# GpSimd's low halves of q and k, subtracted in three pieces of 192 columns

## The chip, the core and the metric

The kernel runs on one core of a Trainium2 chip. The core has a matrix engine (TensorE; PE in the profile, and PEld for its weight loads), three engines for elementwise work (VectorE or DVE, ScalarE or ACT, GpSimd or POOL) and SyncE (SP), which issues most of the transfers. Each runs its own instructions in program order and waits on semaphores for the others. The metric is the device time of one execution in microseconds; less is better.

## What is computed

Three layers follow each other; the change lies in the first, an attention with a decay of 4 x 8 heads, 576 positions and 64 columns a head:

```
scores = scale * np.matmul(q, k.transpose(0, 1, 3, 2))
log_f = np.log(np.clip(f, 0.0001, 1.0))
cum = np.cumsum(log_f, axis=-1)
decay = cum[:, :, :, None] - cum[:, :, None, :]
causal = np.triu(np.ones((S, S), dtype=bool), k=1)
scores = np.where(causal, -1000000000.0, scores + decay)
scores = scores - np.max(scores, axis=-1, keepdims=True)
attn = np.exp(scores)
attn = attn / (np.sum(attn, axis=-1, keepdims=True) + 1e-09)
return np.matmul(attn, v).astype(np.float32)
```

Its output goes through a mix over positions and a feed-forward layer (512 to 2048 to 512), and through a second attention of four experts of which each position uses two.

## The kernel before

The 32 heads of the first attention are done in 16 pairs, one head to a slot. Products on TensorE take operands in two parts, a high one and what it leaves out (the low one), and add three products. ScalarE rounds q and k of a head to the high part (L895 to L899); GpSimd subtracts it from the value (L950 in `split_low`: `qb` for q, then `kb` for k, each 64 partitions by 576 columns), and SyncE's queue copies parts to the other partitions. The values lie in one of two places, `aside` (even pairs) and `room` (odd pairs), that are loaded again (L877) once the subtractions have read them. The parts are made a pair ahead of their use.

In a head's slot TensorE computes scores (`sc`, L297), in a first part and a second one of three column groups; ScalarE takes exponentials (L317, into `pf` or a part of `aside`) and rounds them to the high part `ph` (L322), VectorE subtracts for the low one (L325). From the eleventh head on GpSimd sets the exponentials above the diagonal to zero in between (the selections, L1076), five a head; in the heads before, a product adds a mask. For the head after next TensorE computes products `ua` and `ub` (L201, L219), whose row maxima VectorE finds (L206, L227: once on `ua`, four times on `ub`); TensorE turns them (`mt`, L233), ScalarE shifts them (`mr`, L239) and the queue writes them as a row of the operand (L243). `ub` uses the PSUM buffers of `sc`, so it waits until the exponentials have been read from them. Products of the feed-forward layer (`hps`, `cps`) fill TensorE's time between.

The order on every engine is written out by a table of times: each step is put at a time of a slot of 8.4 units, the steps are sorted, and each engine's instructions are issued in that order, GpSimd's too. The times only set the order; on the chip an instruction starts when its engine has got to it and its semaphores allow. The steps of a pair's parts:

```
us = 4.9 if h else SLOT + 2.8
put(h, us, split_high, p, j)
put(h, us + 1.2, split_moves, p, j)
put(h, us + 1.2, split_low, p, j)
```

and those of a head's exponentials (time of the exponential, of the high part, of the low part):

```
for n, (te, th, tl) in enumerate(((0.75, 2.3 if select else 1.35, 2.7),
                                  (2.2, 3.35, SLOT + 0.4), (2.75, 4.3, SLOT + 1.15))):
```

So the low parts of the second and third group come in the next slot, behind its row maxima.

Of the kernel before, what the change touches and what calls it, by code (L numbers as in the profile page):

```python
# [15 lines left out]
OP = mybir.AluOpType  # L16
# [3 lines left out]
B, H, S, D = 4, 8, 576, 64  # L20
# [58 lines left out]
def f32(ap):  # L79
    return ap.bitcast(F32)  # L80
# [3 lines left out]
def kernel(  # L84
# [13 lines left out]
    nc = tc.nc  # L98
# [773 lines left out]
    def pair_heads(p):  # L872
        return heads[2 * (p % 2)], heads[2 * (p % 2) + 1]
# [64 lines left out]
    def split_low(p, j, which=(0, 1)):  # L938

        if p >= NPAIR:  # L940
            return
        qa, qb, ka, kb = pair_heads(p)[j]
        tq, tk = places[p % 2][0][:, 0, :], places[p % 2][0][:, 1, :]
        if j == 0:
            todo = ((qb[hi_, :], tq[lo_], qa[lo_, :]), (kb[lo_, :S], tk[lo_], ka[lo_, :S]))
        else:
            todo = ((qb[lo_, :], tq[hi_], qb[hi_, :]), (kb[hi_, :S], tk[hi_], khigh[hi_, :]))
        for n in which:
            dst, src, high = todo[n]
            nc.gpsimd.tensor_tensor(dst, src, f32(high), OP.subtract)  # L950

    def one(gen):

# [229 lines left out]
    def split_events(p):  # L1183

        for j in range(2):
            if p < 2:
                for us, do in zip(FIRST_SPLITS[2 * p + j], (split_high, split_moves, split_low)):
                    early(us, do, p, j)
                continue
            h = 2 * (p - 2) + j  # L1190
# [4 lines that stand above are left out]
        if p < 2:  # L1195
            early((1.2, 5.0)[p], load_qk, p)
            early((1.7, 8.6)[p], load_v, p)
            put(0, (0.9, 6.5)[p], load_second, p)
            for j in range(2) if p else ():
                early((10.65, 14.3)[j], put_sums, p, j)  # L1200
            return
        put(*((2 * (p - 2) - 1, 0.1) if p > 2 else (0, -0.05)), load_qk, p)
        put(2 * (p - 2), 2.0 if p > 2 else 8.1, load_v, p)
        if p < NPLAIN:
            put(2 * p - 1, 4.6, load_second, p)
# [964 lines left out]
```

## Time and profile before

| what | value |
|---|---|
| median of 3 runs | 785.31 us (784.35 to 785.93) |
| the profiled execution, its own time | 784.53 us |
| its span (first to last instruction) | 782.8 us |
| around the span | 1.73 us |
| TensorE busy | 757.9 us, 97% of the span |
| GpSimd busy | 202.9 us, 26% of the span |
| first attention | about 10 to 250 us of the span |
| subtractions of L950 | 64, of which 60 from the second pair on |

The profile is of one execution. Busy time is the time in which an engine had an instruction under way, matmuls overlap each other, and their ends are modelled.

### The profile page before, as it was taken

The numbers are of one execution on the slowest core, as the hardware profiler recorded it, in microseconds if no ns is written. First come the engines' busy times: TensorE is split into PE (matmuls) and PEld (weight loads), VectorE is DVE, ScalarE is ACT, GpSimd is POOL, SyncE is SP. The second block draws the span as 40 slices with busy tenths as digits, with TensorE's granted clock in tenths as the row PEclk, the third lists the DMA queues.
The fourth block names the chain that finished last, engine by engine and source line by source line (L and its number), as shares of the span: only waits on it lengthen the run. The fifth ranks groups of instructions, "written<-read, shape, count | busy, mean of one in ns | idle before, by whom it ended". The sixth has DMA issues, their size and how long they took to land.

```text
span 782.8 us, 19114 instructions
## 1 busy us (share of the span) xinstructions
PE 757.9 (97%) x7312; PEld 645.3 (82%) x7312; DVE 601.8 (77%) x1662; ACT 436.4 (56%) x892; POOL 202.9 (26%) x357
## 2 busy tenths in 40 slices
PE   8898989999999999999999999999999999999997
PEld 4798989989999999877777777777778888878874
DVE  8989999999999859988773685466644688787763
ACT  7689888878787635644331242113312466786663
POOL 9842566666564200000020000000000611111110
PEclk9999999999999999999999999999999999999999
DMA  6667765665663166835223124200103475343322
GB/s 191 185 192 202 219 176 167 184 175 169 178 191 97 64 202 205 260 126 168 67 86 129 54 89 157 107 1 2 62 31 77 120 185 139 77 118 97 92 76 95
DMA packets 65688, 101.97 MB, mean 130 GB/s; under 512 B 8854, under 2 KB 43644, under 8 KB 65596
## 3 DMA queue, kind: packets, MB, share of 16 engines
q1 hardware_dynamic: 65084, 99.49, 43.3%
q8 instruction: 58, 0.95, 0.5%
q10 hardware_dynamic: 512, 1.25, 0.5%
q14 instruction: 34, 0.28, 0.1%
HBM read 53.25 MB, written 23.74 MB: 98 GB/s over the span
## 4 chain that ended last, share of the span: by engine, by line
PE 51%; DVE 3%; ACT 1%; DMA 1%; issue 0%; SPq 0%; ACTq 0%
PE cps L732 17%; PE hps L716 16%; PE pq L1668 6%; PE pv L1712 3%; PE sc L297 3%; PE po L1764 2%; PE ub L219 1%; PE av L353 1%; PE av L357 1%; PE av L355 1%; DMA ust<-udram 1%; PE pos L1764 1%; PE ua L201 0%; DVE ph L325 0%; DVE uam L588 0%
## 5 line engine op out<-in xcount | busy, mean ns | idle before, releaser
L721 ACT ACTIVATE hh<-hps 128x288 f16<-128x288 f32 (+1 forms) x128 | 52.4, 410 | 210.7 <-PE hps L716 185.7
L722 DVE SCALAR_TENSOR_TENSOR hl<-hps,hh 128x288 f16<-128x288 f32 (+1 forms) x128 | 58.2, 454 | 79.5 <-ACT hh L721 79.2
L227 DVE CUSTOM_DVE_ANT_0 ub<-ub,maskm 128x448 f32<-128x448 f32 x192 | 82.3, 429 | 1.8 <-PE ub L219 0.3
L297 PE MATMUL sc<-qa,ka 128*128 128x288 f32 (+4 forms) x288 | 72.0, 310 | 0.0
L738 DVE SCALAR_TENSOR_TENSOR yc<-cps,back,yc 128x288 f32<-128x288 f32 x96 | 49.3, 514 | 24.6 <-PE cps L732 23.0
L297 PE MATMUL sc<-qb,kb 128*128 128x288 f32 (+4 forms) x288 | 63.5, 302 | 0.0
L353 PEld LDWEIGHTS <-ph 128*128 128x128 f16 x645 | 58.9, 97 | 1.2 <-DVE o L434 0.6
L355 PEld LDWEIGHTS <-ph 128*128 128x128 f16 x645 | 59.3, 98 | 0.2
L357 PEld LDWEIGHTS <-ph 128*128 128x128 f16 x645 | 59.3, 97 | 0.0
L1896 POOL TENSOR_SCALAR_AFFINE_SELECT pf<-pf 128x128 f32<-128x128 f32 (+1 forms) x80 | 23.8, 318 | 116.4 <-ACT pf L317 115.8
L297 PEld LDWEIGHTS sc<-qb,kb 128*128 128x128 f32 x288 | 52.3, 188 | 1.5
L325 DVE TENSOR_TENSOR ph<-pf,ph 128x512 f16<-128x512 f32 (+1 forms) x66 | 47.5, 732 | 6.4 <-ACT ph L322 6.4
L206 DVE CUSTOM_DVE_ANT_0 ua<-ua,maskm 128x576 f32<-128x576 f32 x48 | 36.5, 761 | 18.8 <-PE ua L201 12.1
L325 DVE TENSOR_TENSOR ph<-aside,ph 128x512 f16<-128x512 f32 (+1 forms) x63 | 50.7, 817 | 0.1
L297 PEld LDWEIGHTS sc<-qa,ka 128*128 128x128 f32 x288 | 48.8, 190 | 2.0 <-issue 0.4
L317 ACT ACTIVATE aside<-sc 128x512 f32<-128x512 f32 (+1 forms) x63 | 38.7, 618 | 20.4 <-PE sc L297 16.9
L1076 POOL TENSOR_SCALAR_AFFINE_SELECT aside<-aside 128x128 f32<-128x128 f32 (+1 forms) x80 | 39.9, 518 | 38.3 <-ACT aside L317 28.8
L732 PE MATMUL cps<-hh,w16b 128*128 128x288 f16 x256 | 48.3, 286 | 0.3 <-DVE hl L722 0.3
L732 PE MATMUL cps<-hh,w1lf 128*128 128x288 f16 x256 | 48.4, 286 | 0.0
L732 PE MATMUL cps<-hh,w16a 128*128 128x288 f16 x256 | 48.4, 286 | 0.0
L317 ACT ACTIVATE pf<-sc 128x512 f32<-128x512 f32 (+1 forms) x66 | 39.8, 610 | 13.0 <-PE sc L297 9.4
L732 PEld LDWEIGHTS <-w16b 128*128 128x128 f16 x384 | 37.4, 98 | 10.2 <-issue 0.8
(289 smaller groups left out, 2469.5 us busy)
## 6 DMA issues: line engine op xcount, KB each, us to landing
raw<-in_w_dram SPq DMA_DIRECT2D x32, 512.0 KB
ust<-udram SPq DMA_DIRECT2D x13, 576.0 KB
ydram<-yc SPq DMA_DIRECT2D x10, 576.0 KB
aside<-in_qk_dram SPq DMA_DIRECT2D x8, 576.0 KB
udram<-ustage SPq DMA_DIRECT2D x16, 288.0 KB
ydram<-ust SPq DMA_DIRECT2D x8, 576.0 KB
yc<-ydram SPq DMA_DIRECT2D x8, 576.0 KB
room<-in_qk_dram SPq DMA_DIRECT2D x7, 576.0 KB
```

The costliest lines, as they stand in the source:

```text
L227: nc.vector.tensor_tensor_reduce(ub[:, bk, off:off + w], ub[:, bk, off:off + w], maskm[:, S - w:S], 1.0, NEG, OP.add, OP.max, mx[:, t:t + 1])
L297: nc.tensor.matmul(ps[:, bk, off:off + w], wa, xa, start=bk not in banks[:n], stop=bk not in banks[n + 1:])
L317: nc.scalar.activation(pf[:, 0:S].rearrange("p (c n) -> p c n", c=2) if whole else pf[:, 0:n], view, AF.Exp, scale=ISC)
L325: nc.vector.tensor_tensor(pl[:, o0:o0 + n], pf[:, 0:n], ph[:, o0:o0 + n], OP.subtract)
L353: nc.tensor.matmul(av[:, it, :], ph[:, c:c + P], vh[:, jt, :], start=first, stop=False)
L355: nc.tensor.matmul(av[:, it, 0:64], ph[:, c:c + P], vl[:, jt, :], start=False, stop=False)
L357: nc.tensor.matmul(av[:, it, :], pl[:, c:c + P], vh[:, jt, :], start=False, stop=last)
L716: nc.tensor.matmul(ph[:], wa[:, k, fs], xa[:, k], start=n == 0, stop=n == 3 * KT - 1)
L721: after(lambda: nc.scalar.activation(hh[:], ph[:], AF.Relu), lambda: nc.vector.scalar_tensor_tensor(hl[:], ph[:], 0.0, high, OP.max, OP.su ...
L722: lambda: nc.vector.scalar_tensor_tensor(hl[:], ph[:], 0.0, high, OP.max, OP.subtract))
L732: nc.tensor.matmul(pc[:], wa[:, t, dsl], xa[:], start=n == 0, stop=n == 3 * FT - 1)
L738: nc.vector.scalar_tensor_tensor(yc[:, d, :], pc[:], back, yc[:, d, :], OP.mult, OP.add)
```

## The change

From the second pair on (`p` not 0) each subtraction of 576 columns is issued as three of 192, one behind the other, over the same rows. The first pair keeps its four whole ones. So 60 instructions become 180.

```
+        w = S // 3 if p else S
         for n in which:
             dst, src, high = todo[n]
-            nc.gpsimd.tensor_tensor(dst, src, f32(high), OP.subtract)
+            for c in range(0, S, w):
+                nc.gpsimd.tensor_tensor(dst[:, c:c + w], src[:, c:c + w], f32(high[:, c:c + w]),
+                                        OP.subtract)
```

On GpSimd, in the slots of the heads with selections, there stood before (names of buffers, then partitions and columns):

```order
L950 TENSOR_TENSOR qb_135<-room,qa_134 64x576
L950 TENSOR_TENSOR kb_137<-room,ka_136 64x576
L1076 AFFINE_SELECT aside<-aside 128x128 x3
L1076 AFFINE_SELECT pf<-pf 128x128
L1076 AFFINE_SELECT pf<-pf 128x64
L950 TENSOR_TENSOR qb_139<-room,qb_139 64x576
L950 TENSOR_TENSOR kb_141<-room,khigh 64x576
```

and now, at the same place, with every line number behind the change three higher:

```order
L952 TENSOR_TENSOR qb_135<-room,qa_134 64x192 x3
L952 TENSOR_TENSOR kb_137<-room,ka_136 64x192 x3
L1079 AFFINE_SELECT aside<-aside 128x128 x3
L1079 AFFINE_SELECT pf<-pf 128x128
L1079 AFFINE_SELECT pf<-pf 128x64
L952 TENSOR_TENSOR qb_139<-room,qb_139 64x192 x3
L952 TENSOR_TENSOR kb_141<-room,khigh 64x192 x3
```

Nothing moved past anything else: the six pieces stand where the two subtractions stood, ahead of the same selections.

On TensorE, in the second part of a head's scores, the order is the same and two products have got a wait of their own, since they read columns of later pieces than the first part did:

```order
L297 MATMUL sc<-qa_138,ka_140 128x448
L297 MATMUL sc<-qb_139,kb_141 128x320 [waits Pool_49]
L297 MATMUL sc<-qb_139,kb_141 128x192 [waits Pool_49]
L297 MATMUL sc<-qb_139,kb_141 128x448
L297 MATMUL sc<-qa_138,ka_140 128x64
```

Before, these rows stood without a wait, since the first part had waited for the whole tile.

## Rows read from the trace of the kernel before

**Rows 1.** Stretches: us, busy of PE, PEld, DVE, ACT, POOL, clock, DMA.

```profile
18.00:120.00 102.00, 94.14 (x970) 85.57 (x968) 95.49 (x282) 84.68 (x172) 56.62 (x57) 1.00 0.69 197
120.00:240.00 120.00, 116.06 (x1353) 110.66 (x1352) 114.78 (x323) 96.08 (x190) 75.76 (x99) 1.00 0.60 174
```

**Rows 2.** Waits of weight loads, 18 to 280 us: total, times, longest.

```profile
PEld mt L233 <- DVE mx L227: 11.6, 20, 1.6
...
PEld ub L219 <- ACT aside L317: 3.3, 4, 1.3
```

**Rows 3.** VectorE's waits, 0 to 250 us: total, times, longest.

```profile
DVE ua L206 <- PE ua L201: 6.8, 12, 1.0
```

**Rows 4.** VectorE in order of time: start us, us.

```profile
29.63 0.39 DVE L461 SCALAR_TENSOR_TENSOR u<-ur,u 128x160 int32<-128x160 int32 x1
30.05 1.46 DVE L462 SCALAR_TENSOR_TENSOR u<-ur,u 128x160 int32<-128x160 int32 x1
31.43 1.72 DVE L407 SCALAR_TENSOR_TENSOR vw<-room,rs,vw 128x320 f16<-128x320 f32 x1
...
34.33 0.74 DVE L325 TENSOR_TENSOR ph<-aside,ph 128x576 f16<-128x576 f32 x1
```

**Rows 5.** GpSimd in order of time, the same stretch.

```profile
29.91 1.41 POOL L950 TENSOR_TENSOR qb<-aside,qb 64x576 fp32r<-64x576 f32 x1
31.40 1.41 POOL L950 TENSOR_TENSOR kb<-aside,khigh 64x576 fp32r<-64x576 f32 x1
...
34.18 2.17 POOL L950 TENSOR_TENSOR qb<-room,qa 64x576 fp32r<-64x576 f32 x1
```

**Rows 6.** VectorE elsewhere, with no subtraction on GpSimd beside it.

```profile
74.74 0.55 DVE L407 SCALAR_TENSOR_TENSOR vw<-aside,rs,vw 128x320 f16<-128x320 f32 x1
...
201.06 0.68 DVE L325 TENSOR_TENSOR ph<-aside,ph 128x512 f16<-128x512 f32 x1
```

**Rows 7.** GpSimd, one slot with selections.

```profile
137.91 1.40 POOL L950 TENSOR_TENSOR qb<-room,qb 64x576 fp32r<-64x576 f32 x1 [1.50 <-issue]
139.39 1.42 POOL L950 TENSOR_TENSOR kb<-room,khigh 64x576 fp32r<-64x576 f32 x1
140.89 0.63 POOL L1076 TENSOR_SCALAR_AFFINE_SELECT aside<-aside 128x128 f32<-128x128 f32 x1
...
143.21 0.48 POOL L1076 TENSOR_SCALAR_AFFINE_SELECT aside<-aside 128x128 f32<-128x128 f32 x2
```

**Rows 8.** VectorE: low parts behind `kb`, in that slot and two others.

```profile
51.91 1.08 DVE L325 TENSOR_TENSOR ph<-pf,ph 128x512 f16<-128x512 f32 x1
...
140.28 1.08 DVE L325 TENSOR_TENSOR ph<-aside,ph 128x512 f16<-128x512 f32 x1
...
141.28 0.77 DVE L325 TENSOR_TENSOR ph<-aside,ph 128x512 f16<-128x512 f32 x1
...
243.09 1.06 DVE L325 TENSOR_TENSOR ph<-aside,ph 128x512 f16<-128x512 f32 x1
```

**Rows 9.** Groups of GpSimd's instructions by shape: count, busy us, mean ns.

```profile
L950 POOL TENSOR_TENSOR kb<-aside,ka 64x576 fp32r<-64x576 f32 x8 | 11.3, 1412 | 0.6
...
L1076 POOL TENSOR_SCALAR_AFFINE_SELECT aside<-aside 128x64 f32<-128x64 f32 x15 | 4.0, 264 | 0.0
...
L1300 POOL TENSOR_TENSOR vs<-vst,vs 32x288 fp32r<-32x288 f32 x2 | 1.6, 794 | 2.8 <-ACT vs L1296 2.7
```

**Rows 10.** GpSimd, first selections of two other slots.

```profile
116.52 0.28 POOL L1076 TENSOR_SCALAR_AFFINE_SELECT aside<-aside 128x128 f32<-128x128 f32 x1
...
243.67 0.63 POOL L1076 TENSOR_SCALAR_AFFINE_SELECT aside<-aside 128x128 f32<-128x128 f32 x1
```

**Rows 11.** ScalarE and TensorE in the slot of the 140.28 low part.

```profile
141.96 0.66 ACT L322 CAST ph<-aside 128x576 f16<-128x576 f32 x1
142.52 0.60 ACT L317 ACTIVATE aside<-sc 128x512 f32<-128x512 f32 x1
...
143.19 0.74 PE L219 MATMUL ub<-ka,qa 127*128 127x448 f32 x4
```

## Prediction

> **What bounds the kernel now.** The page's busy shares are averages over stages, so I read the stage of the change by itself, in the busy times by stretch. In the first attention VectorE is as full as TensorE: 95.49 of 102 us and 114.78 of 120 us, where TensorE has 94.14 and 116.06; GpSimd has 56.62 and 75.76 [rows 1]. What the change is worth is made there and then passed on, since none of its 60 subtractions stands behind 245 us and the engines' order behind them is the same.
>
> Then the waits. TensorE waits chiefly for VectorE: 20 times and 11.6 us for the last row maximum; four times and 3.3 us it waits for ScalarE's exponentials to free the buffer of `ub` [rows 2]. VectorE in turn waits 12 times, 6.8 us in all, for the products of `ua` [rows 3], one product group to each of 32 heads. The two run in step. GpSimd is not full, but what it does holds the others in two ways, which the next parts show from the rows in order of time.
>
> **What a subtraction does to VectorE.** At 29.63 an integer operation L461 takes 0.39 us; L462, of the same shape, starts at 30.05 and takes 1.46 [rows 4]. GpSimd's `qb` runs from 29.91 to 31.32 [rows 5], and L462 ends at 31.51, 0.19 us behind it. The next one, L407, takes 0.55 us in a free place [rows 6] and 1.72 here: GpSimd's `kb` came in at 31.40, and L407 ends 0.34 us behind its end at 32.81. At 140.28 a low part L325 takes 1.08 us instead of 0.68 and ends at 141.36, 0.55 us behind `kb` [rows 6, 7, 8]. The reading: a VectorE operation with two inputs in SBUF does its last part, about 0.2 to 0.55 us by its length, only when GpSimd's subtraction is over; and when GpSimd has another ready, the two take turns, one instruction each. [...]
>
> **The price of a piece.** No L950 of 192 columns is in the trace. Two shapes of the same operation are: 576 columns take 1412 ns, 288 take 794 [rows 9]. That is 618/288 = 2.15 ns a column and 176 ns for each instruction, so 192 columns take 588 ns. Two selections that follow each other, of 128 and of 64 columns, take 0.48 us together [rows 7], where one of each apart takes 0.28 [rows 10] and 0.26 [rows 9]; so I let a next piece start 0.05 early: 0.588 + 2 x 0.54 = 1.67 us for three, 0.26 more than one whole, 0.52 for `qb` and `kb`. Bounds: no price at all for an instruction (0.47 a piece, nothing added), and the 0.07 us that lie between `qb` and `kb` [rows 5] ahead of each piece (0.66 a piece, 0.5 added for each three). I take the middle one, since the 288 columns are the nearest row.
>
> **Early slots, where something is gained.** I work through the turns from 29.91. The first piece ends at 30.50, so L462 ends 0.19 behind it, at 30.69 instead of 31.51. The second piece takes its turn, of which VectorE sees some 0.45 us, and L407 ends 0.34 behind it, at 31.48 instead of 33.15: 1.67 us gained. But four pieces are left, and two of the next operations of VectorE have two inputs in SBUF again, another L462 and the low part of 34.33 [rows 4]; before, they ran with no subtraction beside them. Each waits for a piece, 2 x 0.45, and 0.77 us are left. What TensorE waits for most are maxima that stand behind such operations on VectorE [rows 2], so I let TensorE gain all of it: **-0.8** (bounds: nothing, and -1.67).
>
> **Low parts that come behind `kb`.** From 51.9 to 243.1 us there are 14 places where a low part of the second group, or the low part of the feed-forward input, is held behind `kb`; the first, the last and the one at 140.28 are shown [rows 8], and in all 14 the held operation starts within 1 us of `kb`'s start, as there by 0.89 [rows 7]. I work through the one of `qb` at 137.91 [rows 7]. `qb` in pieces ends at 139.58, `kb` begins at 139.65, its second piece runs to 140.78. The low part ends 0.55 behind that, at 141.33, where it ended at 141.36: nothing is gained, since the pieces have pushed `kb` back. The third piece takes its turn from 141.33 to 141.78, and now the second low part, which took 0.77 right behind the first [rows 8], has to wait: it ends 0.55 behind the piece, at 142.33 instead of 142.05. VectorE is 0.28 us later, where it should be earlier. VectorE's own idle time swallows it in 12 of 32 heads [rows 3]; in 9 of the 14 places (five belong to the next part) I count 9 x 0.28 x 20/32 = **+1.6** (bounds: 0, and 9 x 0.45 = 4).
>
> **Selections that come right behind `kb`.** The first selection at 140.89 stands right behind `kb` and ended at 141.52 [rows 7]. In pieces, and behind the second low part, it ends at about 142.48, 0.96 later. ScalarE's rounding of that group began at 141.96 [rows 11], so 0.44 is covered and ScalarE is 0.52 late; queued behind it is the exponential of 142.52, and when that ended at 143.12 TensorE's `ub` could start at 143.19. There is no slack in that chain: `ub` goes to about 143.7. Of the 18 slots with both subtractions and selections, 7 have no gap between `kb` and the selection, the first at 116.52 and the last at 243.67 [rows 10]; the others have gaps that hide some or all of it. TensorE would have waited for the next maximum in most heads anyway [rows 2], and that maximum is itself only 0.28 late; so each of the 7 costs between 0.28 and 0.52, and I take 0.35: **+2.45** (bounds: 0, and 7 x 0.96 = 6.7).
>
> **What costs nothing.** TensorE's new waits are for pieces made a head or more before. The queue's load of `room` or `aside` waits for the same subtractions and comes up to 1 us later, with the row of the maxima behind it on the same queue; that row waits longer for ScalarE in the slots I looked at. If that cover fails it is 0.52 us, the added length of `qb` and `kb`, in an early head, inside the range.
>
> **Sum.** -0.8 + 1.6 + 2.45 = +3.25 us on the profiled execution's 784.53: 787.8. The median of the runs is 785.31, so I predict 788.6. A measurement of this kernel can tell about 0.2% from no change, 1.6 us.
>
> **The rivals.** *Cheap pieces, faster.* If an instruction's price is hidden, three pieces take 1.41 us, `kb` ends when it did, and VectorE only waits less. For: consecutive instructions overlap a little [rows 7]; against: the 794 ns of half the columns [rows 9]. The early slots then give -1.67, and half of the 14 places some 0.2 less, -1.4 x 20/32 = -0.9: 785.31 - 2.6 = 782.7. It decides below about 0.5 us a piece. [...] I give this 0.20.
>
> *No difference.* VectorE's and ScalarE's lateness goes into waits that are there, and the early gain meets the rest. For: the 6.8 us of waits [rows 3]; against: `ub` with no slack [rows 11]. 785.3, within 1.6; 0.20.
>
> *Much slower.* [...] If that is what happens at each turn, each later piece waits for a whole row of VectorE operations, a selection comes another 0.5 us later and ScalarE with it: 7 x 0.5 on top of the 3.25, 6.75, and 785.3 + 6.5 = 791.8 with a little of it hidden; 0.13.
>
> The forecast itself, 786.9 to 790.5, has 0.47. For the range I leave out the outer halves of the first and last rival: 783.2 to 791.8. Faster by over 0.2%: 0.20; within: 0.22; slower: 0.58.
>
> **What would show it.** In the profile after: pieces of 0.55 to 0.6 us; L462 and L407 at 30 us at well under 1 us each; the two low parts in slots like 140 us both over 0.68; first selections later behind the subtractions; more wait of ScalarE for GpSimd and of `ub` for ScalarE; TensorE ahead of before at 50 us and behind it at 250 us, and the same from there on. Pieces under 0.5 us, or low parts at 0.68 with GpSimd beside them, would make it wrong.

## The result: 793.25 us, slower

The changed kernel takes 793.25 us in the median of six runs (790.59 to 794.83), the kernel before 785.01 in as many (784.35 to 789.45). The ratio is 1.010, with a 95% interval of 1.0085 to 1.0115: 8.2 us slower. I had predicted 788.6, and at most 791.8. The direction was right; more than half of the loss was missing from the sum. Two of the six runs, 790.59 and 791.5, lie under 791.8, the median does not.

### The profile page after: what moved, and what is told of

It reads as the page before. It is cut to its first block, busy times and chain, and to the rows that moved or that the text cites. A ratio compares the mean times of both kernels' runs of the same rounds, so it can differ in the third digit from the quotient of the medians.

```text
span 791.6 us, 19238 instructions
## 1 busy us (share of the span) xinstructions
PE 761.0 (96%) x7312; PEld 646.6 (82%) x7312; DVE 609.2 (77%) x1662; ACT 437.5 (55%) x892; POOL 231.6 (29%) x477
## 4 chain that ended last, share of the span: by engine, by line
PE 51%; DVE 3%; ACT 1%; DMA 1%; issue 0%; SPq 0%; ACTq 0%
PE cps L732 17%; PE hps L716 15%; PE pq L1671 6%; PE pv L1715 3%; PE sc L297 3%; PE po L1767 2%; PE ub L219 1%; PE av L353 1%; PE av L357 1%; PE av L355 1%; DMA ust<-udram 1%; PE pos L1767 1%; PE ua L201 0%; DVE ph L325 0%; DVE uam L588 0%
## 5 line engine op out<-in xcount | busy, mean ns | idle before, releaser
L325 DVE TENSOR_TENSOR ph<-aside,ph 128x512 f16<-128x512 f32 (+1 forms) x63 | 54.4, 875 | 1.1 <-ACT ph L322 0.9
L325 DVE TENSOR_TENSOR ph<-pf,ph 128x512 f16<-128x512 f32 (+1 forms) x66 | 50.2, 774 | 6.4 <-ACT ph L322 6.4
```

Source lines behind the costliest of these rows:

```text
L325: nc.vector.tensor_tensor(pl[:, o0:o0 + n], pf[:, 0:n], ph[:, o0:o0 + n], OP.subtract)
```

## The profile after

The page of the changed kernel, its span and its busy times:

```profile
span 791.6 us, 19238 instructions
PE 761.0 (96%) x7312; PEld 646.6 (82%) x7312; DVE 609.2 (77%) x1662; ACT 437.5 (55%) x892; POOL 231.6 (29%) x477
```

The profiled executions differ by 791.6 - 782.8 = 8.8 us. GpSimd is busy for 28.7 us more: 60 subtractions that grew by the price of the pieces alone, 0.26 us each, would make 15.6. So the pieces cost GpSimd more than their price: 146 of the 180 take under 0.65 us, and the other 34 add 13.9 us beyond 0.59 each.

Busy time by stretch, as [rows 1]:

```profile
18.00:120.00 102.00, 91.99 (x942) 83.13 (x939) 93.52 (x274) 82.59 (x167) 66.65 (x111) 0.98 0.68 192
120.00:240.00 120.00, 113.42 (x1314) 107.38 (x1315) 116.22 (x308) 93.83 (x184) 88.06 (x151) 1.00 0.58 167
```

TensorE does 942 matmuls in the first stretch where it did 970, and the granted clock, 1.00 before, is 0.98. The waits of weight loads from 18 to 280 us, as [rows 2]:

```profile
PEld mt L233 <- DVE mx L227: 10.4, 18, 2.1
PEld up L983 <- DVE g L971: 6.2, 12, 1.0
PEld ub L219 <- ACT aside L317: 6.1, 8, 1.6
PEld ub L219 <- ACT pf L317: 3.2, 5, 1.2
PEld sc L297 <- DVE u L462: 2.3, 1, 2.3
```

In the kernel before, the row of `up` in the same view was:

```profile
PEld up L980 <- DVE g L968: 4.5, 13, 0.9
```

The wait for the maxima did not grow. What grew is `ub` behind ScalarE's `aside` (3.3 to 6.1 us), `up` behind VectorE's `g`, and a single wait of 2.3 us that is new. The profile puts that one down to VectorE's `u`; where the lag comes from shows when it is followed along the program. Three of TensorE's instructions serve as posts, each named by its start in the kernel before: the turned maxima that stood at 38.19 us, the first `hps` product of 96.06, and the first score product of 249.71. Their start in each kernel's profiled execution, less the start before (the lag):

```
kernel                          38.19   96.06  249.71
changed kernel                  +2.54   +3.41   +8.73
a1  pieces from pair 2 on       -1.34   -0.38   +6.44
a2  pieces in pair 1            +0.74   +0.73   +0.68
a3  pieces in pairs 2 to 6      -1.34   -0.38   -0.44
c1  load behind the row         -0.03   +1.28   +7.82
d3  pieces in pairs 1 to 6      +1.09   +1.97   +2.00
a4  pieces from pair 7 on       +0.03   +0.04   +5.24
b5  two writes from pair 7 on   -0.05   -0.05   +1.77
```

So 2.5 us are lost by 38 us, 0.9 up to 96 and 5.3 up to 250; behind that the lag changes little, 8.5 at 260 us and 9.0 at 700. At the first post TensorE waited in the kernel before:

```profile
38.19 0.27 PE L233 MATMUL mt<-ident,mx 128*5 128x128 f32 x1 [1.24 <-DVE mx L227]
```

The experiments take these parts one by one.

**Up to 38 us.** GpSimd's last subtraction for pair 1, and SyncE's queue behind it; first both in the kernel before, then after:

```profile
22.05 1.41 POOL L950 TENSOR_TENSOR kb<-room,khigh 64x576 fp32r<-64x576 f32 x1
```

```profile
24.29 0.38 SPq L877 DMA_DIRECT2D room<-in_qk_dram  x1
24.76 0.80 SPq L243 DMA_DIRECT2D qa<-mr  x1
```

```profile
23.11 2.74 POOL L952 TENSOR_TENSOR kb<-room,khigh 64x192 fp32r<-64x192 f32 x3
```

```profile
25.87 0.35 SPq L877 DMA_DIRECT2D room<-in_qk_dram  x1
26.31 0.80 SPq L243 DMA_DIRECT2D qa<-mr  x1
```

The subtraction ended at 23.46 and ends at 25.85. The load of `room` starts 0.02 us behind the last piece; the row of the maxima stands behind it and is 1.55 us later than before. TensorE's scores that read this row started at 28.29 before, 3.5 us behind its issue; they start 4.4 behind it now (4.2 in a2), so the transfer took longer too, which nothing here explains:

```profile
30.73 0.37 PE L297 MATMUL sc<-qa,ka 128*128 128x288 f32 x1 [2.20 <-DVE u L462]
```

And the stretches from 28 to 36 us after (columns as in [rows 1]; before, the clock is 1.00 in all of them):

```profile
28.00:30.00 2.00, 0.53 (x18) 0.40 (x14) 1.99 (x10) 1.94 (x5) 1.94 (x5) 1.00 0.87 272
30.00:32.00 2.00, 1.27 (x6) 0.94 (x7) 1.97 (x5) 0.28 (x2) 1.94 (x4) 0.78 0.78 180
32.00:34.00 2.00, 2.00 (x9) 1.60 (x7) 1.21 (x3) 1.35 (x3) 1.94 (x3) 0.50 0.33 75
34.00:36.00 2.00, 2.00 (x20) 1.96 (x19) 0.68 (x1) 0.98 (x3) 1.94 (x5) 0.87 0.39 99
```

TensorE stands still for 2.2 us, and behind that its granted clock is 0.78, 0.50 and 0.87: 9 matmuls from 32 to 34 us.

**VectorE at 30 us**, as [rows 4], and GpSimd beside it:

```profile
30.10 0.60 DVE L462 SCALAR_TENSOR_TENSOR u<-ur,u 128x160 int32<-128x160 int32 x1
30.62 0.90 DVE L407 SCALAR_TENSOR_TENSOR vw<-room,rs,vw 128x320 f16<-128x320 f32 x1
```

```profile
28.75 1.76 POOL L952 TENSOR_TENSOR kb<-aside,ka 64x192 fp32r<-64x192 f32 x3
30.57 2.15 POOL L952 TENSOR_TENSOR qb<-aside,qb 64x192 fp32r<-64x192 f32 x3
```

They end at 30.70 and 31.52; I had worked out 30.69 and 31.48. That the times agree so well is luck. I had let `qb`'s pieces begin at 29.91, but the two subtractions ahead of them are in pieces too, and they begin at 30.57: L462 ends 0.19 us behind the last piece of the `kb` before (30.51), and L407 0.36 behind `qb`'s first (31.16), not its second. The lags of 0.19 and 0.34 are what holds. The gain that I forecast is there, but TensorE is behind by then.

**The slot of 140 us**, the place of [rows 7, 8, 11], at a lag of 4.7 us. GpSimd, VectorE, ScalarE and TensorE after:

```profile
142.93 1.72 POOL L952 TENSOR_TENSOR qb<-room,qb 64x192 fp32r<-64x192 f32 x3 [1.48 <-issue]
144.73 2.60 POOL L952 TENSOR_TENSOR kb<-room,khigh 64x192 fp32r<-64x192 f32 x3
147.40 0.76 POOL L1079 TENSOR_SCALAR_AFFINE_SELECT aside<-aside 128x128 f32<-128x128 f32 x1
```

```profile
145.01 1.86 DVE L325 TENSOR_TENSOR ph<-aside,ph 128x512 f16<-128x512 f32 x2
146.79 1.22 DVE L407 SCALAR_TENSOR_TENSOR vw<-aside,rs,vw 128x640 f16<-128x640 f32 x1
```

```profile
148.19 0.67 ACT L322 CAST ph<-aside 128x576 f16<-128x576 f32 x1 [1.42 <-POOL aside L1079]
```

```profile
149.41 0.77 PE L219 MATMUL ub<-ka,qa 127*128 127x448 f32 x4 [1.34 <-ACT aside L317]
```

The durations of `kb`'s three pieces there (least, median, most), and of the two low parts:

```profile
L952 POOL TENSOR_TENSOR kb<-room,khigh x3: 592/1042/1046, 144.7 to 146.3; 64x192 fp32r<-64x192 f32 x3
```

```profile
L325 DVE TENSOR_TENSOR ph<-aside,ph x2: 860/968/1075, 145.0 to 145.8; 128x512 f16<-128x512 f32 x2
```

This is the view to learn from. `qb`'s three pieces together, with nothing beside them, take 1.72 us; the first of `kb`'s takes 0.59. The second and third take 1.04 each: VectorE's low part goes between two pieces, and the piece waits for it as it waits for the piece. Behind the whole `kb` one low part ended 0.55 us after it [rows 7, 8]; now the first low part ends 0.55 us behind the first piece (145.87 against 145.32), the second 0.55 behind the second (146.87 against 146.32), and GpSimd pays 0.45 us for each of the two waits inside `kb`. `kb` ends at 147.33, the selection at 148.16, and less the lag of 4.7 this is 1.9 us later than in [rows 7], where I had 0.96: 0.5 is the price of both operands' pieces, 0.9 are the two waits, 0.3 a later start of `qb`, and 0.1 the selection's own longer time. ScalarE waits 1.42 us for it and TensorE's `ub` 1.34 behind that. The hold works both ways: the low parts take 0.86 and 1.08 us, and a piece loses 0.45 us to a low part that takes 0.68 alone [rows 6], less than the whole of that operation's time.

## The experiments

Each kernel is the changed one but for the lines shown, and is timed beside the kernel before on the same chip.

### Where in the program the loss is made

```
a1   w = S // 3 if p > 1 else S
a2   w = S // 3 if p == 1 else S
a3   w = S // 3 if 1 < p < 7 else S
```

c1, the order on SyncE's queue:

```
-        put(*((2 * (p - 2) - 1, 0.1) if p > 2 else (0, -0.05)), load_qk, p)
+        put(*((2 * (p - 2) - 1, 1.35 if p == 3 else 0.1) if p > 2 else (0, -0.05)), load_qk, p)
```

**a1, pair 1 whole.**

> Pair 1's four subtractions stay whole, pieces from pair 2 on. Theory Q: of the 8.2 us that the change cost, about 2.5 come from pair 1 alone: its pieces end 2.4 us later, the queue's load of room (L877) waits for them, and the row of the maxima (L243) stands behind that load, so TensorE's scores at 28 us come late. Then this runs at about 790.7, with no stall of TensorE at 28 us. Rival U: the loss is spread evenly over the 60 subtractions, 0.14 us each; then 792.7.

Measured: 790.86 us, ratio 1.009 (1.0068 to 1.0112), and at 28 us TensorE is 0.06 us from where it was, as Q has it. That the time is Q's as well is in part luck: at the post of 96.06 this execution is 3.8 us ahead of the changed kernel's, since the early gain comes back too, and 1.6 of that is lost again at 118 us to a fall of the granted clock (third column from the end) that the changed kernel's execution did not have:

```profile
116.42 0.27 PE L233 MATMUL mt<-ident,mx 128*5 128x128 f32 x1 [1.85 <-DVE mx L227]
```

```profile
118.00:120.00 2.00, 2.00 (x11) 2.00 (x10) 1.74 (x4) 2.00 (x4) 1.09 (x4) 0.52 0.44 93
```

**c1, the load behind the row.**

> All pieces as in the changed kernel; only the queue's load of room for pair 3 is put behind the row of the maxima instead of ahead of it. Theory Q: the row no longer waits for the pieces, the stall at 28 us goes, about 790.7. If TensorE waited there for the pieces themselves or for VectorE, nothing changes: 793.2.

Measured: 790.55 us, ratio 1.0079 (1.0066 to 1.0092). The queue:

```profile
23.95 0.79 SPq L243 DMA_DIRECT2D qa<-mr  x1
25.95 0.36 SPq L877 DMA_DIRECT2D room<-in_qk_dram  x1
```

The load still waits for the last piece, and the row no longer does. All the pieces are there, and about 2.2 us of the 8.2 are gone: it was the queue's order that made pair 1's pieces dear. This profiled execution, 1.2 us above the median, has two falls of the clock of its own, at 25 and at 148 us. The first made TensorE 1.1 us later, and at the post of 38.19 it is at -0.03, where a1 has -1.34.

**a2, pair 1 alone.**

> Pieces in pair 1 only, all other subtractions whole. Theory Q: about 787.5, with a stall of 2 us and more at 28 us, a lower granted clock behind it, and the trace unchanged behind 50 us. Rival U: 785.5.

Measured: 784.87 us against 784.47, ratio 1.0013 (1.0004 to 1.0021). Half of Q fails here: the stall is there, and costs only 0.4. TensorE:

```profile
30.56 0.37 PE L297 MATMUL sc<-qa,ka 128*128 128x288 f32 x1 [2.00 <-DMA qa<-mr]
...
38.93 0.27 PE L233 MATMUL mt<-ident,mx 128*5 128x128 f32 x1
```

The scores are 2.3 us late, and here the profile names the row itself as what ended the wait. But the maxima of 38.19, for which TensorE waited 1.24 us before, are only 0.74 us later and without a wait: the stall was paid out of that wait. In the profiled execution the granted clock did not fall there.

**a3, pairs 2 to 6.**

> Pieces in pairs 2 to 6 only (no selections in their slots). In the changed kernel TensorE's lag fell by 1.45 us between 35 and 40 us and rose by 0.85 between 40 and 100. If the fall is the gain that I forecast for the early slots, this runs at 784.4 to 784.9; if the fall was only slack that swallowed the stall, at 785.9. Rival U: 20 subtractions cost 2.7, 787.7.

Measured: 783.96 us against 784.47, ratio 0.9994 (0.9986 to 1.0003). The same maxima:

```profile
36.85 0.27 PE L233 MATMUL mt<-ident,mx 128*5 128x128 f32 x1
```

1.34 us earlier, again without a wait. So the early gain is real, and larger than my 0.8; up to 96 us 0.96 of it is given back. VectorE shows why it is larger, beside [rows 4]:

```profile
32.33 0.74 DVE L462 SCALAR_TENSOR_TENSOR vst<-vraw,vst 96x288 int32<-96x288 int32 x1
32.99 0.74 DVE L325 TENSOR_TENSOR ph<-aside,ph 128x576 f16<-128x576 f32 x1
```

L462 pays 0.28 us (0.46 before) and the low part of 34.33 nothing, where I had taken off 0.45 for each. The low part ends 1.34 us earlier than before, the whole of the gain.

a2 and a3 use the same wait. Then they shouldn't add up.

**d3, pairs 1 to 6** (`w = S // 3 if 0 < p < 7 else S`).

> Pieces in pairs 1 to 6. Pair 1 alone cost 0.4 us, pairs 2 to 6 alone gave 0.5; if their effects add up, this is 784.4, as before. Theory W: both effects use the same wait, the 1.24 us for the maximum at 38 us: pair 1's stall is paid out of it, and the early pieces' gain is its removal, so it can be had once. Then 785 + 2.2 (stall) - 0.1 + 0.85 (the slots up to 100 us) less the little that is left of the wait, about 787, and 1.5 to 1.8 more where the granted clock falls behind the stall.

Measured: 786.48 us, ratio 1.0024 (1.0015 to 1.0033), where the sum of the two would be 784.4. Theory W holds:

```profile
39.28 0.27 PE L233 MATMUL mt<-ident,mx 128*5 128x128 f32 x1
```

```profile
32.00:34.00 2.00, 2.00 (x20) 1.97 (x19) 1.97 (x4) 1.55 (x4) 1.94 (x4) 1.00 0.37 86
```

The maxima are 1.09 us late, with the gain and the stall both in it. In this execution the clock stayed at 1.00 there; in the changed kernel, whose program is the same up to then, it fell, and the same maxima are 2.54 us late. That puts the fall at 1.45 us. The pieces of pairs 1 to 6 with c1's order on the queue, which should have the gain without the stall, were not run.

### What the slots with selections lose, and to what

```
a4   w = S // 3 if p > 6 else S
b2   w = S // 3 if p > 6 and n == 0 else S
b3   w = S // 3 if p > 6 and n == 1 else S
```

b1 and b5 have whole subtractions, and from pair 7 on, behind each of them, three (b1) or two (b5) small writes to a buffer that nothing reads (its allocation and `w = S` are left out here):

```
+            if p > 6:
+                for _ in range(2):
+                    nc.gpsimd.memset(padt[0:64, :], 0.0)
```

**a4, pieces from pair 7 on.**

> Pieces only from pair 7 on, whose subtractions stand ahead of selections. With pieces everywhere TensorE's lag rose from 3.4 us at 95 us to 8.5 at 250. Theory S: these slots carry the loss by themselves, 5.1 us: about 789.6, and 791 if TensorE's granted clock falls once behind one of the longer waits, as it did at 118 us with pieces from pair 2 on (about 1.5 us). Rival: the lag of the early slots is what makes the later ones late; then under 788.

Measured: 789.47 us against 784.25, ratio 1.0072 (1.0055 to 1.0089). These slots carry their loss by themselves, 5.2 us. The pieces of one of the operands there:

```profile
L952 POOL TENSOR_TENSOR kb<-aside,khigh x12: 592/811/1417, 124.5 to 230.8; 64x192 fp32r<-64x192 f32 x12
```

Of all 108 pieces there 89 take under 0.65 us, and the other 19 add 8.6 us beyond 0.59 each. The price, 36 x 0.26 = 9.4 us, is as much again.

**b1, three writes.**

> Whole subtractions; from pair 7 on GpSimd writes zeros into a small buffer of its own three times behind each, about 0.3 us, a little more than the three pieces are longer than one whole. No turn is added, only the time. Theory P: the loss is the price of the added instructions, which makes the selections late; then about as slow as pieces from pair 7 on, 789 to 790. Theory T: it is the turns that VectorE takes between the pieces; then about half or less of it, 786 to 787.5.

Measured: 788.2 us, ratio 1.0056 (1.0041 to 1.0071). It falls between the two theories, and it was not the control that it should be: the writes take 0.43 us where 0.3 was meant.

**b5, two writes.**

> As the kernel with whole subtractions and small writes of zeros behind them from pair 7 on, but two writes, not three. The three took 0.38 to 0.48 us of GpSimd a subtraction and cost 3.9 us; two should take 0.25 to 0.35, as much as the three pieces add (0.26 to 0.31). Theory P (the time alone): about as slow as pieces from pair 7 on, 789. Theory T (turns besides): in proportion to the three writes, 2.7 us, about 787, and what is left to 5.2 is the turns'.

Measured: 787.13 us against 784.59, ratio 1.0033 (1.0019 to 1.0047). GpSimd in the 140 us slot:

```profile
138.32 1.41 POOL L953 TENSOR_TENSOR qb<-room,qb 64x576 fp32r<-64x576 f32 x1 [1.50 <-issue]
139.67 0.27 POOL L957 MEMSET padt<- 64x16 f32 x2
140.01 1.43 POOL L953 TENSOR_TENSOR kb<-room,khigh 64x576 fp32r<-64x576 f32 x1
141.50 0.27 POOL L957 MEMSET padt<- 64x16 f32 x2
141.83 0.31 POOL L1083 TENSOR_SCALAR_AFFINE_SELECT aside<-aside 128x128 f32<-128x128 f32 x1
```

From `qb`'s start to the selection's are 3.51 us, against 2.98 in [rows 7]: 0.53 added, as much as the price of the pieces for both subtractions (0.52). The same time without turns costs 2.5 us in the median (1.8 by the post of 249.71), the pieces 5.2. So a third to a half of the loss of these slots is the price, and the rest the turns, as theory T has it. The slot of 140 us shows the difference best: between 136 and 148 us a4's lag grows by 1.62 us and b5's by 0.21. But the writes match the pieces only up to the start of the selection, which then takes 0.31 us here and 0.63 in [rows 7], and single times run from 785.99 to 791.96; the shares are rough.

**b2, q alone; b3, k alone.**

> From pair 7 on only q's subtraction is in three pieces, k's is whole. Theory T: q's pieces mostly run with no two-input operation of VectorE beside them and only push k's back by 0.3 us, 785.5 to 786.5. Theory P: half of the loss of pieces from pair 7 on, about 787.5.

Measured: 786.6 us, ratio 1.0033 (1.002 to 1.0046).

> From pair 7 on only k's subtraction is in three pieces, q's is whole. Theory T: most of the loss of pieces from pair 7 on, 788 to 789.5, with k's three pieces taking 2 us and more together where VectorE's low parts stand. Theory P: half of the loss, about 787.5.

Measured: 787.37 us, ratio 1.0039 (1.0024 to 1.0054). b2 lies at the upper end of theory T's range; b3 is against theory T, which had 788 to 789.5 for it, and fits P's 787.5. q's pieces run nearly free (0.60 us each) and still cost 2.3 us, so the added time hurts by itself; k's are the stretched ones, `kb` from `khigh` 0.75 and 0.89 us in the mean, and cost 3.1 us in the median, less than the "most of the loss" that T expected. In the medians the two make 5.5 us, as much as a4; at the post of 249.71, in single executions, they lag 2.01 and 1.92, together 1.3 less. So time and turns both count, and these two runs do not settle in what shares.

### Is there a version that keeps the gain?

```
d1   w = S // 3 if p == 2 else S
d2   w = S // 3 if p in (2, 3) else S
```

**d1, pair 2.**

> Pieces in pair 2 only. If the early gain is the shorter hold of VectorE at 30 to 33 us, TensorE's wait at 38 us goes and nothing is given back later: 783.1 to 783.4, faster than before. If pair 3's pieces have their part in it, 784 or more.

Measured: 784.09 us against 784.59, ratio 0.9989 (0.998 to 0.9998): faster, by 0.1%, and not the 783.1 to 783.4 of the first case. The 1.3 us are there at 38 us, but 1.1 are gone by 45. GpSimd, VectorE, and VectorE in the kernel before:

```profile
36.32 1.41 POOL L952 TENSOR_TENSOR qb<-room,qa 64x576 fp32r<-64x576 f32 x1
37.80 1.73 POOL L952 TENSOR_TENSOR kb<-room,ka 64x576 fp32r<-64x576 f32 x1
```

```profile
37.08 3.00 DVE L325 TENSOR_TENSOR ph<-aside,ph 128x512 f16<-128x512 f32 x2
```

```profile
38.39 1.43 DVE L325 TENSOR_TENSOR ph<-aside,ph 128x512 f16<-128x512 f32 x2
```

Pair 2's pieces end later than its whole subtractions did, so pair 3's whole ones now meet two low parts, which take 3.00 us together where they took 1.43.

**d2, pairs 2 and 3.**

> Pieces in pairs 2 and 3. Pieces in pairs 2 to 6 gave 1.3 us at 38 us and lost 0.9 between 60 and 100; pair 3's subtractions stand at 34 to 46 us, so this one gains as pair 2 alone does: 783.1 to 783.4.

Measured: 783.27 us against 784.59 in the median, ratio 0.9989 (0.9974 to 1.0003). It keeps the gain (the low parts take 1.92). But two of its twelve executions took 787.65 and 787.93 us, at a mean granted clock of 0.992 where the others have 0.996 and more. The profiled one is among them; its stretches, with the clock in the third column from the end:

```profile
76.00:78.00 2.00, 1.30 (x7) 1.28 (x8) 2.00 (x4) 2.00 (x5) 0.00 (x0) 0.74 0.45 104
78.00:80.00 2.00, 2.00 (x12) 2.00 (x11) 1.64 (x9) 1.97 (x5) 1.56 (x2) 0.50 1.03 386
...
84.00:86.00 2.00, 2.00 (x13) 1.91 (x12) 1.97 (x5) 0.00 (x0) 0.00 (x0) 0.50 0.01 1
```

In the median it is 1.3 us under the kernel before, but the interval takes in no difference, so a gain is not shown.

## Why the prediction was wrong, step by step

- **VectorE behind a subtraction: right.** It ends 0.19 and 0.36 us behind a piece, where I had 0.19 and 0.34. That the ends at 30.70 and 31.52 us are those worked out is luck, since they stand behind other pieces than I had.
- **The price of a piece: right.** 0.59 us forecast, 0.59 measured for a piece with nothing beside it, and 1.72 for `qb`'s three at 140 us where I had 1.67.
- **The early gain: right in kind, too small.** I had -0.8; a3 shows -1.34. I took off 0.45 for each of two operations and wrote that no subtraction stood beside them before; but `qb` of 34.18 did stand beside the low part of 34.33 [rows 4, 5], and in a3 the two pay 0.28 together. In the changed kernel it can't be had, because it is the removal of the wait at 38 us, and the stall ahead of it uses up that wait (d3).
- **"What costs nothing": the step that failed.** I had seen that the queue's load waits for the subtractions with the row of the maxima behind it, and bounded it by 0.52 us, the price of one pair's `qb` and `kb`. But four subtractions stand one behind the other there, 1.0 us by their price, and VectorE's turns came on top: the last one ended 2.4 us later (25.85 against 23.46). The row, issued 1.55 us later, came too late for the scores, and TensorE stood still for 2.2 us. With the early gain in it this cost +1.1 (d3) instead of -0.8, and the fall of the granted clock another 1.45. Together 3.3 us of the miss.
- **Low parts and selections: the right places, mis-sized.** I had 1.6 + 2.45 = 4.05 us; the lag grew by 0.87 from 38 to 96 us and by 5.32 up to 250, 6.2. I had let one piece of `kb` wait for VectorE, the third. Two did: the first low part got in behind the first piece already, not behind the second. In the 140 us slot VectorE is hardly later (the second low part ended at 142.05 before and at 146.87 now, 0.1 us later less the lag), and GpSimd is 0.8 us later with `kb` than I had it, its selection nearly 1.0. The loss went through ScalarE to `ub`, as forecast, and not through the maxima, whose wait did not grow. TensorE's products `up`, which I had not named, wait for VectorE 6.2 us where they waited 4.5.
- **The rivals.** The last one, *much slower*, named the nearest time, 791.8, with another cause. It took from `qb` of 34.18, which needed 2.17 us while a low part ran in its 0.74 [rows 4, 5], that a whole row of VectorE's operations goes ahead of each later piece, with 0.5 us more at each of seven selections. No run shows this 0.5 us; in its place the 140 us slot has 0.9, two pieces of 1.04 us with one operation of VectorE ahead of each. One piece of a3 does wait for two: `kb`'s first at 32.81 us takes 1.38 of the 2.48 that its three take there, behind both L462 and the low part shown above. *Cheap pieces* falls with the 0.59 us: it needed less than about 0.5.

In sum, the profiled execution lost 8.8 us: 1.1 by pair 1's stall less the early gain, 1.45 by the clock, 0.9 in the slots without selections, 5.3 in those with them. By b5 a third to a half of the 5.3 is the time of the added instructions and the rest the turns; b3 does not bear that share out, so it stays open.

## What to carry to other kernels

Where two engines take turns as VectorE and GpSimd do here, cutting one's instruction shortens each wait of the other (L462 from 1.46 us [rows 4] to 0.60) and adds a turn for itself (0.45 us for each of two pieces of `kb`): cost both sides, and look at what stands behind the cut one (here a selection, and a queue). Bound a hidden cost by all that ends ahead of it, not by the one instruction that was edited. A wait on the critical engine can be used up once: an earlier stall and a later gain that both end in it don't add up (d3 took 786.48 us where the sum was 784.4), so measure them together.

## What was not expected of the hardware

The granted clock of TensorE fell to 0.50 to 0.54, in the lowest 2 us of each fall, for some microseconds in single executions. In the changed kernel it did behind a wait of 2.2 us, and cost 1.45. In a2, behind a wait of 2.0 us, the profiled execution and most others kept the clock (784.7 to 785.2 us), and four of eleven, at mean clocks of 0.996 to 0.998, took 786.5 to 786.8. The length of TensorE's last wait does not decide it, for at each of four falls another kernel's execution has the same wait at the same place of the program and keeps the clock:

```
fell: run, us, wait ahead       kept: run, wait
changed kernel, 30     2.20     d3               2.22
a1, 118                1.85     changed kernel   1.83
d2, 77                 0.97     a3               0.96
c1, 25                 0.94     changed kernel   0.94
```

The fall in d2 lasted longest, some 10 us, and made its lag 4.4 us larger; that of a1 cost 1.6, that of c1 at 25 us 1.1. A second fall in c1, at 148 us behind 1.84, has no such partner. What decides whether the clock falls stays open.
